# Half-width score products and an output one pair behind, in a gated linear attention with a squared-ReLU feed-forward

## The chip, the cores and the metric

One core of one Trainium2 chip runs the whole program in one launch. The metric is the device time of that core in microseconds (us). Engine names are those of the profile: PE is TensorE (PEld its weight loads), DVE is VectorE, ACT is ScalarE, POOL is GpSimd, SP issues the DMAs.

## The reference

```python
# q, k, v, alpha: (4 batches, 8 heads, 768 steps, 48), fp32; alpha in 0.8..1
for t in range(768):
    state = alpha[:, :, t, :, None] * state + einsum('bhd,bhe->bhde', k[:, :, t], v[:, :, t])
    y[:, :, t] = einsum('bhd,bhde->bhe', q[:, :, t], state)
x = y.transpose(0, 2, 1, 3).reshape(3072, 384)
h = maximum(x @ w_in, 0)          # w_in 384 x 2048, given in 64-bit floats
out = h * h @ w_out               # w_out 2048 x 384
```

The recurrence is computed by blocks of 128 steps of one batch (24 blocks: block n is batch n % 4, chunk n // 4). With b the running product of alpha in the block, q is multiplied by b and k by 1/b; then y = q·S + (masked scores)·v, where S is the state before the block, the scores are k against q, and the mask keeps a step's own and earlier steps. The new state is (S + sum of k·v) times the last b.

## The kernel before

Blocks go in six groups of four; a group's x is then 384 x 512 and goes through both layers of the feed-forward. Group 0 is computed in an opening, written out step by step. The attention of group g+1 is woven between the matmuls of group g's second layer (for group 1: between both layers of group 0). `weave` runs the list of feed-forward units in order and puts an attention step in front of the first unit whose time (a sum of unit costs) has reached the step's. In the groups from 1 on, the second layer has 28 units of four products each.

A head has 48 columns, two heads fill 128 rows as two halves of 64 (`e` = 0, 1), four such pairs `p`. From block 4 on, the scores of a block leave out one square of 64 x 64 (later keys against earlier queries): the first 64 keys meet all 128 queries, the last 64 keys only the last 64. The products use quarters of the PE array (64 rows x 64 columns). So that all four quarters work, the halves of some heads are swapped in place, and v is also loaded with its halves exchanged (`w`, 40 small DMAs). In the listing `chunks` and `halves_of_s` place the pieces; `sc` are the scores, `am` the masked copy to SBUF, `y` the output with the state sums `kv`, `st` the state, and `ev` copies y to x.

```python
    def bank(n, name, shape=(NP, C)):
        if n < GB and name in ("sc", "y"):
            return ps_ffn.tile([128, *shape], FP32, tag="f", name=name)
        return ps_att.tile([128, *shape], FP32, tag="att", name=name)
# ...
    def sc(n):
        ps = blk[n]["sc"] = [bank(n, "sc") for _ in range(2)]
        ks, qs = blk[n]["ks"], blk[n]["qs"]
# ...
        for x in range(2):
            for i in range(2):
                for p in (x, NP // 2 + x):
                    for e in range(2):
                        half = halves_of_s(p, i)
                        rows = slice(64 * e, 64 * e + D)
                        t = slice(64 * i, C)
                        nc.tensor.matmul(
                            out=chunks(ps[e].rearrange("a p t -> a (p t)"), half, p, i),
                            lhsT=ks[rows, p, 64 * i : 64 * (i + 1)], rhs=qs[rows, p, t],
                            start=True, stop=True, skip_group_check=True,
                        )
# ...
    def am(n):
        ps = blk[n].pop("sc")
# ...
        for e in range(2):
            o, data = (
                x.rearrange("a p t -> a (p t)")[:, 0 : 3 * C].rearrange("a (x k) -> a x k", x=2)
                for x in (am_t[n % NAM][:, e], ps[e])
            )
            mask = parts.rearrange("a k t -> a (k t)").bitcast(U32)
            nc.vector.copy_predicated(
                out=o, mask=mask.unsqueeze(1).to_broadcast(list(o.shape)), data=data
            )
# ...
    def y(n):
        ns, ys = [n, n + 1], [bank(n, "y", (2, NP // 2, C)) for _ in range(2)]
# ...
        heads = [(m, p, e) for m in ns for p in range(NP) for e in range(2)]
        for m in ns:
            blk[m]["y"] = ys
        for m, p, e in heads:
            if m // B:
                rows = slice(64 * e, 64 * e + D)
                product(m, p, e, s_t[m % B][rows, p, 0 : D + G * e], blk[m]["qs"][rows, p, :])
        if n < GB:
# ...
        for phase in range(2):
            for m in ns:
                for i in range(2):
                    for row in (1 - phase, phase) if (m, i) == (ns[0], 0) else (0, 1):
                        e = row ^ phase
                        for p in range(NP):
                            half = halves_of_s(p, i)
                            if half.start != 64 * row:
                                continue
                            x, h = "v", 2 * p + e
                            if p >= NP // 2:
                                x, h = "w", h - H // 2
                            cols = slice(h * D - G * e, (h + 1) * D)
                            ins = product(
                                m, p, e, tiles[x][m % len(tiles[x])][half, cols],
                                chunks(
                                    am_t[m % NAM][:, e].rearrange("a p t -> a (p t)"), half, p, i
                                ), slice(64 * i, C),
                            )
                            order("y", ins, phase)
            pass_on("y")
            for m in ns:
                if m // B == NCH - 1:
                    continue
                if phase == 0 and m == n:
                    kv = [bank(n, "kv", (2, NP // 2, 64)) for _ in range(2)]
                    begun = set()
                for p in range(NP):
                    half = slice(64 * (p % 2 ^ phase), 64 * (p % 2 ^ phase) + 64)
                    for e in range(2):
                        first = (2 * p + e) * D - G * e
                        ins = nc.tensor.matmul(
                            out=kv[p % 2][64 * e : 64 * (e + 1), m % 2, p // 2, :],
                            lhsT=tiles["k"][m % 4][half, 2 * p + e, :],
                            rhs=tiles["v"][m % NV][half, first : first + 64],
                            start=(p % 2, e) not in begun, stop=True, skip_group_check=True,
                        )
                        begun.add((p % 2, e))
                        order("kv", ins, phase)
                blk[m]["kv"] = kv
# ...
        else:
            s = s_t[n % B]
            for x in range(2):
                o = s[:, x::2, :]
                nc.vector.tensor_tensor(out=o, in0=src[x][:, n % 2], in1=o, op=ALU.add)
            nc.vector.tensor_tensor(
                out=s, in0=s, in1=last_t[n % 4].unsqueeze(2).to_broadcast([128, NP, 64]),
                op=ALU.mult,
            )
```

Between the two phases of `y` the rows of the array change the PSUM bank that they write; the `passed` instruction, an empty one on POOL, makes the second phase wait for the first. `ps_att` has four PSUM banks for the attention, taken in turn: a step that asks for a bank waits until the step four banks before it has been read.

The schedule:

```python
    PLAN = (
        (0.0, "ln0 ln1"),
        (2.0, "cs0 eb0 ei0"),
        (3.5, "cs1 mk0 eb1 ei1"),
        (5.0, "mq0 mq1 mk1"),
        (6.0, "kT0 kc0 bl0 bl1"),
        (7.0, "qT0 qc0 qT1 qc1"),
        (8.0, "kT1 kc1 br0 br1"),
        (10.0, "sc0 sc1 am0"),
        (11.0, "am1"),
        (12.0, "y0 ev0 st0 st1"),
    )
# ...
    def attention(g, begin, scale):
        out = []
        for at, fs in PLAN:
            for f in fs.split():
                for t in begin:
                    n = GB * g + 2 * begin.index(t) + int(f[-1])
                    out.append((t + at * scale, steps[f[:-1]], (n,)))
                    if f[:-1] == "qT" and n + 2 < NBLK:
                        out.append((t + at * scale, load, (n + 2, "aq")))
# ...
    def weave(units, events):
        at = 0
        for cost, f, args in units:
            while events and events[0][0] <= at:
                _, e, given = events.pop(0)
                e(*given)
            f(*args)
            at += cost
        for _, e, given in events:
            e(*given)
# ...
    units += [(1, ffn_out, (0, t, i)) for i in range(NW) for t in range(GB)]
    events = [(4.0 * i, next_weights, ()) for i in range(2 * NW)] + [(0, load, (GB + 1,))]
    events += [(47 + 2 * r, sum_w_in, (r,)) for r in range(NR2 - 1)]
    events += attention(1, (2.0, 27.0), 2.1)
    events += [(53, sum_x, (1,)), (54, sum_w_in, (NR2 - 1,))]
    weave(units, sorted(events, key=lambda x: x[0]))
    for g in range(1, NG):
        for j in range(NJ // 2 + 1):
            for i, step in enumerate("ABacCDd"):
                if j - step.islower() in range(NJ // 2):
                    ffn_in_pair(g, j - step.islower(), step)
# ...
        if g + 1 < NG:
            events = attention(g + 1, (0, 12.0), 1) + [(NU - 3, sum_x, (g + 1,))]
        weave([(1, ffn_product, (g, *divmod(u, NR2))) for u in range(NU)], events)
```

## Time and profile before

| | |
|---|---|
| time, median of 3 runs | 575.7 us (575.4 to 576.33) |
| span of the profiled execution | 573.2 us |
| PE, DVE, ACT busy | 560.3, 327.6, 222.8 us |
| opening (group 0's attention), to about 38 us | PE busy 29.9 of 38 |
| both layers of group 0 with group 1's attention | 38.2 to 132.3 us |
| first layer of each later group | 38.0 us each |
| second layer with attention, groups 1, 2, 3, 4 | 52.9, 52.9, 52.9, 51.7 us |
| second layer of group 5, no attention | 36.4 us |
| DMA | 38.94 MB, of it 1.9 MB the exchanged v |

The stretches are read off the chain of work that ended last, in order of time: its pieces are start, length, engine, tile, line and the number of instructions. In this trace one product in fp32 is two instructions, so "o x16" are eight products. A group of instructions by shape gives the busy time and the mean of one; because products in different quarters overlap, a mean is a latency there, and the pace has to be taken from the length of a piece divided by its instructions.

### The profile page before, as it was taken

To read this page: it belongs to the slowest core of one execution; us is meant where nothing else is said; L and a number is where in the kernel's file an instruction comes from. 1 tells how busy PE (TensorE), PEld (TensorE's weight loads), DVE (VectorE), ACT (ScalarE), POOL (GpSimd) and SP (SyncE) were. 2 spreads that over 40 slices of the span, in tenths; PEclk is the share of its full clock that TensorE was granted. 3 is DMA by queue.
4 is the path that set the end of the run, shared out by engine and by line. 5 is a ranking of instruction groups with operands and counts; after the bars stand their busy time and mean duration, and the time that the engine had idled before them with its cause. 6 is when DMAs were issued, how large, how long until landed. Compare 5 with 4: busy or idle time off the path is not lost.

```text
span 573.2 us, 11429 instructions
## 1 busy us (share of the span) xinstructions
PE 560.3 (98%) x4756; PEld 481.0 (84%) x4756; DVE 327.6 (57%) x653; ACT 222.8 (39%) x493; POOL 4.5 (1%) x29
## 2 busy tenths in 40 slices
PE   8789999999999999999999999999999999999996
PEld 6654565668889999889999888999988999988996
DVE  4988669875874534664534565652566443366430
ACT  4459865432344323334343234242333432333100
POOL 3000000000000000000000000000000000000000
PEclk9999999999999999999999999999999999999999
DMA  9986557621003335000454000435200340100001
GB/s 166 251 187 188 147 126 248 125 42 56 1 1 56 72 56 125 1 0 16 79 91 98 29 0 2 84 57 102 67 1 1 61 65 1 56 1 1 1 1 55
DMA packets 127963, 38.94 MB, mean 68 GB/s; under 512 B 119700, under 2 KB 122792, under 8 KB 127912
## 3 DMA queue, kind: packets, MB, share of 16 engines
q1 hardware_dynamic: 127912, 38.22, 30.5%
q8 instruction: 37, 0.61, 0.5%
q14 instruction: 14, 0.11, 0.1%
HBM read 33.45 MB, written 4.75 MB: 67 GB/s over the span
## 4 chain that ended last, share of the span: by engine, by line
PE 96%; DVE 2%; DMA 1%; issue 0%; ACT 0%; SPq 0%; POOL 0%; POOLq 0%
PE h L649 33%; PE o L720 32%; PE o L686 7%; PE h L611 7%; PE y L416 5%; PE cs L260 3%; PE sc L349 3%; PE qT L303 2%; PE kT L303 2%; PE kv L490 1%; DMA raw<-in_moe_w_in_dram 1%; PE warm L232 1%; PE sc L335 0%; DVE xT L514 0%; PE kv L393 0%
## 5 line engine op out<-in xcount | busy, mean ns | idle before, releaser
L649 PE MATMUL h<-xT,w_in 128*128 128x256 f32 x480 | 124.0, 379 | 0.0
L649 PEld LDWEIGHTS h<-xT,w_in 128*128 128x128 f32 x480 | 91.1, 190 | 12.3
L720 PE MATMUL o<-w_out,hid 128*128 128x192 f32 x480 | 83.3, 327 | 0.0
L720 PEld LDWEIGHTS o<-w_out,hid 128*128 128x128 f32 x480 | 78.7, 190 | 3.7
L514 ACT COPY xT<-y 32x256 f32<-32x256 f32 (+2 forms) x132 | 46.2, 364 | 77.1 <-PE y L416 73.5
L662 DVE TENSOR_TENSOR hid<-h,u 128x256 f32<-128x256 f32 x120 | 50.8, 424 | 28.9 <-PE h L649 25.0
L667 ACT ACTIVATE hid<-hid 128x256 f32<-128x256 f32 x40 | 16.7, 417 | 114.6 <-DVE hid L662 114.6
L662 DVE TENSOR_TENSOR u<-h,u 128x256 f32<-128x256 f32 x80 | 33.8, 423 | 35.3 <-PE h L649 22.9
L649 PE MATMUL h<-s3x,ws 128*128 128x256 f32 x160 | 47.6, 379 | 0.0
L611 PE MATMUL h<-xT,w_in 128*128 128x512 f32 (+1 forms) x108 | 43.6, 550 | 3.3 <-ACT xT L514 1.8
L384 DVE COPY_PREDICATED am<-parts,sc 128x384 f32<-128x384 uint32 x40 | 20.6, 577 | 45.7 <-PE sc L349 45.6
L686 PE MATMUL o<-w_out,hid 128*128 128x384 f32 x128 | 42.9, 489 | 0.0
L720 PE MATMUL o<-t,s 128*128 128x192 f32 x240 | 42.4, 328 | 0.0
L649 PE MATMUL h<-s3x,w_in 128*128 128x256 f32 x160 | 41.1, 379 | 0.0
L720 PEld LDWEIGHTS o<-t,s 128*128 128x128 f32 x240 | 39.0, 190 | 1.3
L611 PEld LDWEIGHTS h<-xT,w_in 128*128 128x128 f32 x108 | 19.8, 190 | 22.4 <-issue 16.3
L686 PEld LDWEIGHTS o<-w_out,hid 128*128 128x128 f32 x128 | 23.9, 190 | 15.6
L649 PEld LDWEIGHTS h<-s3x,ws 128*128 128x128 f32 x160 | 30.4, 190 | 4.1
L649 PEld LDWEIGHTS h<-s3x,w_in 128*128 128x128 f32 x160 | 30.4, 190 | 4.1
L720 PE MATMUL o<-t,hid 128*128 128x192 f32 x160 | 27.9, 329 | 0.0
L669 DVE SCALAR_TENSOR_TENSOR hid<-hid 128x512 f32<-128x512 f32 x40 | 27.2, 681 | 0.0
L720 PEld LDWEIGHTS o<-t,hid 128*128 128x128 f32 x160 | 25.8, 190 | 0.3
(109 smaller groups left out, 759.2 us busy)
## 6 DMA issues: line engine op xcount, KB each, us to landing
raw<-in_moe_w_in_dram SPq DMA_DIRECT2D x8, 768.0 KB, 5.5
raw<-in_moe_w_out_dram SPq DMA_DIRECT2D x8, 768.0 KB, 4.6
k_in<-in_k_dram SPq DMA_DIRECT2D x24, 192.0 KB, 5.0
out_dram<-osb SPq DMA_DIRECT2D x24, 192.0 KB, 2.1
v_in<-in_v_dram SPq DMA_DIRECT2D x23, 192.0 KB, 5.0
a_in<-in_alpha_dram SPq DMA_DIRECT2D x22, 192.0 KB, 3.6
q_in<-in_q_dram SPq DMA_DIRECT2D x22, 192.0 KB, 3.9
vx_in<-in_v_dram SPq DMA_DIRECT2D x40, 48.0 KB, 2.5
```

What stands on the lines that cost most here:

```text
L260: nc.tensor.matmul(out=ps.rearrange("a p t -> a (p t)")[:, 0 : H * D], lhsT=causal, rhs=blk[n].pop("la"), start=True, stop=True,)
L303: nc.tensor.transpose(out=ps[:, p, :], in_=rows[:, 128 * p : 128 * (p + 1)], identity=ident)
L349: nc.tensor.matmul(out=chunks(ps[e].rearrange("a p t -> a (p t)"), half, p, i), lhsT=ks[rows, p, 64 * i : 64 * (i + 1)], rhs=qs[rows, p, t ...
L384: nc.vector.copy_predicated(out=o, mask=mask.unsqueeze(1).to_broadcast(list(o.shape)), data=data)
L416: ins = nc.tensor.matmul(out=slot(ps)[64 * half : 64 * half + D + G * e, t], lhsT=lhsT, rhs=rhs, start=key not in seen, stop=True, skip_gr ...
L514: copy(out=x[to : to + m, kk, t : t + 2], in_=blk[n]["y"][e][r : r + m, :, p // 2],)
L611: nc.tensor.matmul(out=ps, lhsT=w[:, kk, c0 : c0 + 128], rhs=xT[g][:, kk, cols], start=(kk == 0), stop=(kk == KM - 1),)
L649: nc.tensor.matmul(out=ps, lhsT=a, rhs=b, start=(step.isupper() and i == 0), stop=(i == len(pairs) - 1), skip_group_check=True,)
L662: nc.vector.tensor_tensor(out=o, in0=ps, in1=z, op=ALU.add)
L669: nc.vector.scalar_tensor_tensor(out=h2, in0=h2, scalar=0.0, in1=h2, op0=ALU.max, op1=ALU.mult)
L686: nc.tensor.matmul(out=acc[t][:, 0:DM], lhsT=hid[i][:, j, t * C : (t + 1) * C], rhs=w_out[i][:, j, :], start=(i == 0 and j == 0), stop=(i ...
L720: nc.tensor.matmul(out=acc[k][:, t, :], lhsT=lhs[:, j, t * C : (t + 1) * C], rhs=rhs[:, j, :], start=(first and r + j + t == 0), stop=(r = ...
```

## The change

From block 4 on:

- The scores are computed as two squares on the diagonal only (16 products of 64 columns a block, where there were 8 of 64 and 8 of 128; the square of later keys against earlier queries was left out already). What the first 64 steps give to the last 64 now goes through the state: `u` = S + the sum of k·v over the first half, and the last 64 queries are multiplied with `u`, the first 64 with S. So q·S is split into two products of 64 columns, and the sums of k·v are kept apart by halves, in the last blocks too, where only the first half is needed.
- The output of a pair of blocks is computed one step behind: `ga(a, n)` does scores, sums, mask and state of block n and then the first part of the output of the pair a = n-2; one unit later `gb` does the rest of a's output, then the same for block n+1, then `ev`. The state is no longer updated in place but in tiles that rotate. Where there is no pair behind (after group 0's end), only the first part runs; a "last" slot does only the output.
- The pairs are spread differently: three slots beside group 0's layers (the third with output only), three pairs beside group 1's second layer, and two slots beside each of the next three, the last of which has output only. The scores of blocks 12 and 13, for instance, move from beside group 2 to beside group 1.
- v's exchanged copy and its DMAs go; v gets a fourth buffer, k has three, the logarithm is taken in place.
- In the opening, three products of a zero tile (128 x 256 each, into a bank that the scores of block 2 then overwrite) are put in front of `kv1`, for which PE waits.

The purpose is less PE work for the same output, with the output's inputs ready a whole slot early. The core of the diff, with cuts:

```diff
-    s_t = kept("s", B, [128, NP, 64])
+    s_t = [p2.tile([128, NP, 64], FP32, tag="s", name="s", bufs=B + 2) for _ in range(B)]
...
+    NV = 4
     tiles = {
...
+        "k": kept("k_in", 3, [128, H, 64]), "v": kept("v_in", NV, [128, H * D]),
     }
...
-    lent = {("a", 2): flat(tsum[0][0]), ("a", 3): flat(tsum[0][1]), ("v", 3): flat(tsum[0][2])}
-    for n in (2, 3):
-        t = lent["q", n] = flat(w_out[4 + n])[:, 0 : 64 * H].rearrange("a (h d) -> a h d", h=H)
+    lent = {("a", 2): flat(tsum[0][0]), ("a", 3): flat(tsum[0][1])}
...
-            if x == "v" and n >= GB:
-                t = tiles["w"][n % 2].rearrange("a (h d) -> a h d", d=D)
-                for i in range(2):
-                    s0 = c * C + (1 - i) * C // 2
-                    nc.sync.dma_start(
-                        out=t[64 * i : 64 * (i + 1)],
-                        in_=v[b, H // 2 :, s0 : s0 + C // 2, :].rearrange("h s d -> s h d"),
-                    )
     raws = {}
...
+    def zeros(n):
+        blk[n]["sc"] = [bank(n, "sc") for _ in range(2)]
+        for _ in range(3):
+            nc.tensor.matmul(
+                out=blk[n]["sc"][0][:, 0:2, :], lhsT=s_t[3].rearrange("a p d -> a (p d)")[:, 0:128],
+                rhs=s_t[3].rearrange("a p d -> a (p d)"), start=True, stop=True,
+            )
     def sc(n):
-        ps = blk[n]["sc"] = [bank(n, "sc") for _ in range(2)]
...
+        blk[n]["y"] = ys
+        def product(m, p, e, lhsT, rhs, t=slice(0, C)):
+            half = e ^ p % 2
+            ins = nc.tensor.matmul(
+                out=ys[e][64 * half : 64 * half + D + G * e, m % 2, p // 2, t], lhsT=lhsT, rhs=rhs,
+                start=(half, e) not in seen, stop=True, skip_group_check=True,
+            )
+            seen.add((half, e))
+            return ins
+        return product
...
+    def scores(n):
+        ps = two[n] = [bank(n, "sckv", (2, NP, 64)) for _ in range(2)]
+        ks, qs = blk[n]["ks"], blk[n]["qs"]
+        for p in range(NP):
+            for h in range(2):
+                for e in range(2):
+                    rows = slice(64 * e, 64 * e + D)
+                    nc.tensor.matmul(
+                        out=ps[e][HALF[h], 0, p, :], lhsT=ks[rows, p, HALF[h]],
+                        rhs=qs[rows, p, HALF[h]], start=True, stop=True, skip_group_check=True,
+                    )
+    def masked(n):
+        ps = two[n]
+        if n // 2 < GB // 2 + NAM and n % 2 == 0:
+            nc.gpsimd.memset(am_t[n // 2 % NAM], 0.0)
+        for e in range(2):
+            nc.vector.copy_predicated(
+                out=am_h(n)[:, e, n % 2], data=ps[e][:, 0],
+                mask=halves_mask.bitcast(U32).unsqueeze(1).to_broadcast([128, NP, 64]),
+            )
+    def am_h(n):
+        t = am_t[n // 2 % NAM].rearrange("a e p t -> a (e p t)")
+        return t.rearrange("a (e m p t) -> a e m p t", e=2, m=2, p=NP)
+    def state_sums(n):
+        ps = two[n]
+        for p in range(NP):
+            for e in range(2):
+                first = (2 * p + e) * D - G * e
+                for h in range(1 if n // B == NCH - 1 else 2):
+                    nc.tensor.matmul(
+                        out=ps[h][64 * e : 64 * (e + 1), 1, p, :],
+                        lhsT=tile_of("k", n)[HALF[h], 2 * p + e, :],
+                        rhs=tiles["v"][n % NV][HALF[h], first : first + 64],
+                        start=True, stop=True, skip_group_check=True,
+                    )
+    def sums_copied(n):
+        ps = two.pop(n)
+        u = blk[n]["u"] = p2.tile([128, NP, 64], FP32, tag="us", name="us", bufs=3)
+        nc.vector.tensor_tensor(out=u, in0=ps[0][:, 1], in1=s_t[n % B], op=ALU.add)
+        blk[n]["kv1"] = ps[1][:, 1]
+    def next_state(n):
+        blk[n]["s"] = s_t[n % B]
+        if n // B < NCH - 1:
+            s = s_t[n % B] = p2.tile([128, NP, 64], FP32, tag="s", name="s", bufs=B + 2)
+            last = last_t[n % 4].unsqueeze(2).to_broadcast([128, NP, 64])
+            nc.vector.tensor_tensor(out=s, in0=blk[n].pop("kv1"), in1=blk[n]["u"], op=ALU.add)
+            nc.vector.tensor_tensor(out=s, in0=s, in1=last, op=ALU.mult)
...
+    def inner(product, m, p, e, h):
+        head = 2 * p + e
+        return product(
+            m, p, e, tiles["v"][m % NV][HALF[h], head * D - G * e : (head + 1) * D],
+            am_h(m)[HALF[h], e, m % 2, p, :], HALF[h],
+        )
...
+    def ga(a, n):
+        if n is not None:
+            for f in (scores, state_sums, masked, sums_copied):
+                f(n)
+        if a is not None:
+            product = y_begin(a)
+            for h in range(2):
+                for m, p, e in heads(a):
+                    rows = slice(64 * e, 64 * e + D)
+                    s = blk[m]["u" if h else "s"]
+                    product(m, p, e, s[rows, p, 0 : D + G * e], blk[m]["qs"][rows, p, HALF[h]], HALF[h])
+            for m, p, e in heads(a):
+                end = inner(product, m, p, e, e)
+            passed = nc.gpsimd.nop(nofuse=True)
+            dep(passed, end)
+            two["y"] = product, passed
+        if n is not None:
+            next_state(n)
+    def gb(a, n):
+        if a is not None:
+            product, passed = two.pop("y")
+            for i, (m, p, e) in enumerate(heads(a)):
+                begin = inner(product, m, p, e, 1 - e)
+                if i == 0:
+                    dep(begin, passed)
+        if n is not None:
+            for f in (scores, state_sums, masked, sums_copied, next_state):
+                f(n + 1)
+        if a is not None:
+            ev(a)
+            for m in (a, a + 1):
+                blk[m].clear()
     def ev(n):
...
+        weights1 y0 cs3 ev0 br1 kT2 qT2 zeros2 ei3 kc2 qc2 kv1 eb3 mk3 load4v kT3 first0
         st0 mq3 weights2 load4q load4k middle0 sc2 kc3 qT3 second0 qc3 bl3 am2 br3 st1 br2
         kv2 sc3 am3 ha0 first1 ha1 middle1 y2 ev2 load4a hb0 first2 hb1 second1 st2 kv3
...
-        (0.0, "ln0 ln1"),
+        (0, "ln0"),
+        (0.5, "ln1"),
         (2.0, "cs0 eb0 ei0"),
-        (3.5, "cs1 mk0 eb1 ei1"),
-        (5.0, "mq0 mq1 mk1"),
-        (6.0, "kT0 kc0 bl0 bl1"),
-        (7.0, "qT0 qc0 qT1 qc1"),
-        (8.0, "kT1 kc1 br0 br1"),
-        (10.0, "sc0 sc1 am0"),
-        (11.0, "am1"),
-        (12.0, "y0 ev0 st0 st1"),
+        (3.0, "cs1 eb1 ei1"),
+        (3.5, "mk0"),
+        (4.0, "bl0"),
+        (4.5, "mq0 mk1 bl1"),
+        (5.0, "mq1"),
+        (6.5, "qT0 qc0 qT1 qc1 kT1 br1"),
+        (7.5, "kc1"),
+        (8.0, "kT0 kc0 br0"),
+        (9.5, "ga"),
+        (10.5, "gb"),
     )
...
     units += [(1, ffn_out, (0, t, i)) for i in range(NW) for t in range(GB)]
-    events = [(4.0 * i, next_weights, ()) for i in range(2 * NW)] + [(0, load, (GB + 1,))]
+    events = [(4.0 * i, next_weights, ()) for i in range(2 * NW)]
+    events += [(0, load, (GB + 1,)), (1.0, load, (GB + 2, "k"))]
     events += [(47 + 2 * r, sum_w_in, (r,)) for r in range(NR2 - 1)]
-    events += attention(1, (2.0, 27.0), 2.1)
+    events += attention([(0, GB, False), (18.0, GB + 2, True), (27.5, GB + 4, True, True)], 2.35)
     events += [(53, sum_x, (1,)), (54, sum_w_in, (NR2 - 1,))]
     weave(units, sorted(events, key=lambda x: x[0]))
     for g in range(1, NG):
...
         if g + 1 < NG:
-            events = attention(g + 1, (0, 12.0), 1) + [(NU - 3, sum_x, (g + 1,))]
+            n = GB * (g + 1) + 2
+            pairs = [(0, n, True), (13.5, n + 2, True)]
+            if g == 1:
+                pairs = [(0, n - 2, False), (7.0, n, True), (14.0, n + 2, True)]
+            events = attention(pairs, 1) + [(NU - 3, sum_x, (g + 1,))]
         weave([(1, ffn_product, (g, *divmod(u, NR2))) for u in range(NU)], events)
```

## The prediction

> **What bounds the kernel now.** I read the page first: how busy is each engine?
>
> ```profile
> PE 560.3 (98%) x4756; PEld 481.0 (84%) x4756; DVE 327.6 (57%) x653; ACT 222.8 (39%) x493; POOL 4.5 (1%) x29
> ```
>
> PE is busy in 98% of the span. Then the waits of PE alone: if it nearly never waits, only less PE work can shorten the program.
>
> ```profile
> PE h L611 <- ACT xT L514: 1.8, 3, 1.3
> PE kv L393 <- DVE ks L319: 1.8, 1, 1.8
> PE kT L303 <- DVE k_in L278: 1.3, 1, 1.3
> PE warm L232 <- POOL s L79: 1.1, 1, 1.1
> PE h L611 <- DVE am L371: 0.9, 1, 0.9
> PE qT L303 <- DVE w_out L278: 0.7, 1, 0.7
> PE h L611 <- DVE w_in L188: 0.6, 1, 0.6
> PE y L416 <- DVE am L371: 0.2, 1, 0.2
> ```
>
> All of these lie before 38.3 us (the list for the window from 38 us on has only the 0.6). From then to the last output PE stands in a queue of its own work. So the change is priced in PE time, piece by piece. The pieces are in the chain in order of time (start, length, engine, tile, instructions); one pair beside group 1's second layer:
>
> ```profile
> 183.69 2.60 PE o L720 x16
> 186.30 1.50 PE sc L349 x64
> 187.79 2.80 PE o L720 x16
> 190.59 1.70 PE y L416 x63
> 192.29 0.47 PE kv L490 x32
> 192.76 0.66 PE y L416 x32
> 193.42 0.47 PE kv L490 x32
> 193.89 2.80 PE o L720 x16
> 196.69 0.65 PE cs L260 x2
> ```
>
> The reader is to see three things. First, sixteen feed-forward instructions take 2.60 us, but 2.80 after a stretch of quarter-array products: coming back costs **0.20 us**. Second, the quarter products of 64 columns run at 0.47/32 = **14.7 ns an instruction** (`kv`). Third, those of 128 columns cost twice as much: `y` has 95 instructions listed (one record is missing), 64 of 128 columns and 32 of 64, so 64 x 29.4 + 32 x 14.7 = 2.35 us, against 1.70 + 0.66 = 2.36 measured. `sc` has 32 of each: 1.41 us, against 1.50 measured; I call the 0.09 left the price of going in.
>
> The means by shape must not be taken for the pace:
>
> ```profile
> L490 PE MATMUL kv<-v_in,k_in 64*64 64x64 f32 x512 | 10.6, 218 | 0.0
> L349 PE MATMUL sc<-qs,ks 48*64 48x128 f32 x320 | 14.5, 277 | 0.0
> ```
>
> 218 ns is the latency of one of many that overlap; the pace is 14.7.
>
> **What the Trainium skill says.** "TensorEngine Tiling (Array Packing)", Key Properties: changing the tiling mode drains the engine. The trace agrees in that 2.60 becomes 2.80. The same page, Gotcha 1: different row tiles cannot access one PSUM bank at the same time. That is why both kernels put a `passed` between the two parts of y; no run here shows what happens without it. "TensorE: Matmul & The Clock Gate", Part 1: after an idle window of about 3.4 us PE falls to half its clock. This is what the zero products guard against. The trace shows half pace only at the start (the warm-up products of 256 columns, 654 ns on average, against 379 for such products later). The hole of 1.8 us does not cost it: `kv` of block 0 and block 2 take 1.03 us for 8, `kv1` right after the hole 1.13, `sc` before and after 1.16 for 16. Nothing to win there.
>
> **The change part by part.** A pair is two blocks.
>
> 1. A pair before: `sc` 1.50, return 0.20, y and kv 1.70 + 0.47 + 0.66 + 0.47 = 3.30, return 0.20. Sum **5.20 us**.
> 2. A pair after, every product with 64 columns and two instructions: scores 2 blocks x 16 products x 2 = 64 instructions; sums 64; state products 16 heads x 2 halves x 2 = 64; inner products 64. Together 256 x 14.7 ns = 3.76 us. There are again two stretches (`ga`, `gb`), so 2 x 0.20 and once 0.09: **4.25 us**. The gain is in two terms: scores 1.41 to 0.94 and inner products 1.41 to 0.94. State products (0.94) and sums (0.94) stay. Ordinary pair: 0.95 us less. Eight such pairs (blocks 4 to 19): -7.6 us.
> 3. The last two pairs (blocks 20 to 23) had no sums before. The chain shows y there at 463.16 us as 1.73 and at 464.98 as 0.89, so 2.71 with the gap; 1.50 + 0.20 + 2.71 + 0.20 = 4.61 us. The change adds sums for the first half: 32 instructions a pair, but on one half of the rows, so two quarters of four, twice the price, and 0.94 us again. After: 4.25. Gain 0.36 x 2 = -0.7 us.
> 4. Extra stretches. Before, five groups x 4 = 20. After, three slots beside group 0, three beside group 1, two beside each of three more: 12 slots x 2 = 24. Four more at 0.20 + 0.09: +1.2 us.
> 5. The rest (transposes, cumulative sums, feed-forward) is the same number of instructions, only moved. The zero products: 6 instructions of 256 columns, at 2.60/16 = 162 ns per 192 columns about 217 each, 1.3 us in a hole that ends 1.8 us after the last qT: fits, 0.
> 6. DVE per block, before: two masked copies of 384 elements at 577 ns, two adds at 283, one product at 425: 2.15 us. After: two masked copies of 256, three tensor operations of 256 at 425. The masked copy is 577 ns at 384 elements and 722 at 512, so 432 at 256 (my estimate from those two). 0.86 + 1.28 = 2.14 us. DVE neither gains nor loses. ACT does the same work. 1.9 MB of small DMAs go, in a program that waits for no DMA after the opening.
>
> Sum: -7.6 - 0.7 + 1.2 = **-7.1 us**, which gives 568.6.
>
> By stretch: both layers of group 0 from 94.0 to about 92.7 us (two pairs less 1.9, two stretches more 0.6); group 1's second layer from 52.9 *up* to 56.5, as it takes a third pair's front (cs 1.3, transposes 1.75 and scores and sums of 1.88); groups 2 and 3 52.9 to 51.0; group 4 51.7 down to 46.1, with one pair's front gone. First layers stay 38.0, the tail 36.4.
>
> **The rivals.**
>
> *A new wait in the dense slots.* Beside group 1 the pairs begin 7 units apart and not 12. `gb` asks for the two banks of `ga`'s scores again, so PE waits unless DVE has masked, added and read the second bank. From the start of `ga`: scores and sums 0.94 us, DVE's four operations behind it end at about 2.4 to 2.9. PE meanwhile has sums, y (1.41) and one unit (2.60/2 + 0.20) and the inner part (0.47): it gets there at 4.3. Without y to do (first slot) it has cs (0.65) instead: at 3.1. Thin but enough. At the end of group 1, `gb` falls on unit 25 of 28: the copies of x take about 12 x 0.364 = 4.4 us, and PE has scores and sums 0.94, the return and three units 3.9, together 5.0, before the first layer needs x. Before, it was four units. Beside group 0 DVE is already busy 33 of 44 us with the weights, in order, so one late operation delays the weights. And k of a block is asked for in `ga`, two units before it is scaled, and lands 5 us later (median): DVE can stall on it. The trace speaks for slack (no PE wait at all after 38.3 us), the plan against it. Each such miss is 0.5 to 2 us; if all came true, the time would be 573 to 575.
>
> *The pace of 14.7 ns does not hold* where 160 instructions with a new weight load each follow one another, or where rows of 48 are used. In y before, 95 + 64 such instructions ran back to back at that pace, so I expect it to hold. If every one cost 17 ns, each pair would lose 0.6 us and the gain would be about 1 us.
>
> *The returns are cheaper than I think.* If the four extra stretches cost nothing: 567.4.
>
> *A shorter opening*: with the exchanged v gone, SP issues the third weight tile 1.4 us earlier. But DVE works through the conversions without a break when PE waits for w_in at 38.2, so I give it nothing.
>
> **Range and chances.** I take 0.6 us of new waits, an estimate for one of the misses above: **569.2 us**. The range of 8 in 10 is 565.5 to 573.5: below, cheaper stretches and a shorter opening; above, several misses. Over 2% faster would be below 564.2, which needs two thirds more than the whole gain I can count: 0.05. Over 2% slower (above 587.2) needs a stall in every slot: 0.03. Within 2%: 0.92.
>
> **What will show it.** In the changed profile: scores, sums, state and inner products at 14.7 ns an instruction, a `ga` of about 2.35 us and a `gb` of about 1.4 with 0.2 behind each; second layers of 56.5, 51.0, 51.0, 46.1 us; PE without waits after 38.3 us; zero products ending before `kv1`'s input is there, and `kv1` where it was. I am wrong if PE waits for DVE or ACT at `sckv`, at `h` after group 1, or if the stretches are longer than their instructions say.

## The result, and the profile after

The changed kernel takes **572.75 us** (median of 3 runs, 572.41 to 572.76) against 575.7: ratio 0.9945, 95% interval 0.9922 to 0.9968. The span of the profiled execution goes from 573.2 to 570.8 us. It is faster by 2.4 to 3 us, less than half of the 6.5 forecast. So the sum of the prediction (-7.1 us in the span) missed by 4.7 us, and the task is to find these.

From the page of after, the line that answers to the one the prediction shows:

```profile
PE 558.5 (98%) x5146; PEld 477.1 (84%) x5146; DVE 326.9 (57%) x655; ACT 222.1 (39%) x493; POOL 5.8 (1%) x28
```

PE has 390 product instructions more (smaller ones; two make a product) and is busy 1.8 us less. DVE and ACT have not moved (327.6 and 222.8 before). So PE is still the bound, as forecast; but where the sum promised 7 us less PE work, there are two. The waits of PE in after from 38 us on (waited for: us in total, times, longest):

```profile
PE h L603 <- DVE w_in L178: 0.6, 1, 0.6
PE sckv L430 <- issue: 0.5, 1, 0.5
PE qT L291 <- DVE q_in L266: 0.3, 1, 0.3
```

The first was there before. The other two are new, and both are longer than this list says, as the chain will show.

The chain of after in order of time (start, length, engine, tile, instructions), one ordinary pair beside group 3's second layer:

```profile
372.40 0.62 PE sckv L404 x32
373.02 0.47 PE sckv L430 x32
373.49 1.40 PE y L380 x90
374.89 1.50 PE o L712 x8
376.39 0.62 PE y L380 x31
377.01 0.47 PE sckv L404 x32
377.48 0.47 PE sckv L430 x32
```

`ga` is 0.62 + 0.47 + 1.40 = **2.49 us** (forecast 2.35), `gb` 0.62 + 0.47 + 0.47 = **1.56** (forecast 1.4); the unit between them is 1.50, which is 1.30 and 0.20 for coming back. The first 32 instructions of each stretch take 0.62, all later ones 0.47: each stretch pays 0.15 us at its ends on top of the 0.20.

The same by stretch. The columns are the window, its length, then the busy time and count of PE, PEld, DVE, ACT and POOL, the granted clock, the DMA share and GB/s. The windows are the second layers of groups 1 to 4, from their first `o` to the first product of the next layer, in after:

```profile
169.66:227.94 58.28, 57.81 (x926) 53.75 (x925) 30.34 (x66) 24.66 (x58) 0.00 (x0) 1.00 0.47 90
265.92:318.21 52.29, 51.84 (x778) 49.38 (x776) 24.79 (x52) 19.88 (x48) 0.00 (x0) 1.00 0.37 70
356.19:407.60 51.41, 51.41 (x745) 49.09 (x744) 23.13 (x48) 19.88 (x48) 0.00 (x0) 1.00 0.34 67
445.59:492.07 46.48, 46.48 (x598) 44.73 (x597) 17.28 (x34) 15.10 (x38) 0.00 (x0) 1.00 0.03 10
```

Groups 2 and 3 have nearly the same work (group 3 has some sums less, worth 0.06 us), but group 2 takes 0.88 us more, and only part of that is idle PE. Forecast were 56.5, 51.0, 51.0 and 46.1. First layers stay at 37.99 and the products of the last layer at 36.41, as before.

Where group 2 loses it, in the chain of after:

```profile
286.74 0.47 PE sckv L404 x32
287.21 0.35 PE sckv L430 x21
287.56 0.45 issue
288.01 0.45 PE sckv L430 x11
```

A run of one kind of product, two thirds done, stops with nothing that it waits for in the profile ("issue"), and comes back slowly: 1.25 us for 32 sums that took 0.47 above.

And group 1, in the timeline of PE and of DVE (start, length, instruction, in brackets the idle time before it and its releaser; the first two lines are PE, the last two DVE):

```profile
195.04 0.63 PE L291 MATMUL qT<-ident,q_in 128*128 128x128 f32 x4
195.98 0.63 PE L291 MATMUL qT<-ident,q_in 128*128 128x128 f32 x4 [0.31 <-DVE q_in L266]
...
194.35 0.55 DVE L266 TENSOR_TENSOR q_in<-q_in,b 128x384 f32<-128x384 f32 x1
195.28 0.55 DVE L266 TENSOR_TENSOR q_in<-q_in,b 128x384 f32<-128x384 f32 x1
```

The scaling of q comes late because DVE is busy without a break from 190.9 us on: to 192.9 with the masks and states of `gb` of the pair in front, then with a scaling of k and two operations of the feed-forward. PE loses 0.50 us before the second transpose (0.94 from start to start, where 0.44 is usual) and, by the same reading, 0.27 before the first: 0.77 together.

### The profile page after: what moved, and what is told of

Same layout as the page of the kernel before. It is cut to its first block, busy times and chain, and to the rows that moved or that the text cites. A ratio compares the mean times of both kernels' runs of the same rounds, so it can differ in the third digit from the quotient of the medians.

```text
span 570.8 us, 12170 instructions
## 1 busy us (share of the span) xinstructions
PE 558.5 (98%) x5146; PEld 477.1 (84%) x5146; DVE 326.9 (57%) x655; ACT 222.1 (39%) x493; POOL 5.8 (1%) x28
## 4 chain that ended last, share of the span: by engine, by line
PE 95%; DVE 2%; DMA 1%; issue 1%; ACT 0%; SPq 0%; POOL 0%; DVEq 0%; POOLq 0%
PE h L641 33%; PE o L712 32%; PE o L678 7%; PE h L603 7%; PE y L380 4%; PE cs L248 3%; PE sckv L404 2%; PE kT L291 2%; PE sckv L430 2%; PE qT L291 2%; DMA raw<-in_moe_w_in_dram 1%; PE warm L220 1%; PE sc L333 0%; DVE xT L520 0%; PE kv L350 0%
## 5 line engine op out<-in xcount | busy, mean ns | idle before, releaser
L520 ACT COPY xT<-y 32x256 f32<-32x256 f32 (+2 forms) x132 | 46.1, 364 | 58.5 <-PE y L380 54.6
L414 DVE COPY_PREDICATED am<-halves_mask,sckv 128x256 f32<-128x256 uint32 x40 | 15.5, 441 | 55.8 <-PE sckv L430 55.8
L661 DVE SCALAR_TENSOR_TENSOR hid<-hid 128x512 f32<-128x512 f32 x40 | 27.3, 681 | 0.0
L746 DVE TENSOR_TENSOR osb<-o,us 128x384 f32<-128x384 f32 x10 | 5.6, 558 | 37.2 <-PE o L712 37.2
```

Of the source, the lines that this page charges most:

```text
L414: nc.vector.copy_predicated(out=am_h(n)[:, e, n % 2], data=ps[e][:, 0], mask=halves_mask.bitcast(U32).unsqueeze(1).to_broadcast([128, NP, ...
L520: copy(out=x[to : to + m, kk, t : t + 2], in_=blk[n]["y"][e][r : r + m, :, p // 2],)
L661: nc.vector.scalar_tensor_tensor(out=h2, in0=h2, scalar=0.0, in1=h2, op0=ALU.max, op1=ALU.mult)
```

## The experiments

The theory (A in the expectations) has three terms: each stretch of quarter products costs 0.35 us beyond its products; PE's instructions run out where very many come in a short time; in the dense slots of group 1 PE waits for DVE. Its rivals: the stops are the DMAs that `gb` starts, or an accident of one run; a stretch costs only the 0.20; or the gain is spent elsewhere (the zero products, the output behind the scores).

**1. The same kernel again.** No edit.

> The changed kernel once more, with more rounds, as the yardstick of the other runs. Both theories: 572.7 us, 0.9945 of the kernel before, with stops of PE in the middle of the quarter-array products of gb at the same places (0.27 us near 222.5 and 0.67 us near 288.0 of the span) if they belong to the program, at others if they are chance.

Measured: 572.07 us, ratio 0.9921 (0.9895 to 0.9947). The stops are at the same products again (at 222.0 us in y, at 286.9 in the sums), with other sizes (0.26 and about 0.08), and there is one of 0.37 at 311.8 that the first profile lacked. So they belong to the program; their size changes from run to run.

**2. `gb` two units after `ga`, beside the second layers.**

```diff
-                    w = t + at * scale
+                    w = t + (at + (f == "gb" and scale == 1)) * scale
...
-                pairs = [(0, n - 2, False), (7.0, n, True), (14.0, n + 2, True)]
+                pairs = [(0, n - 2, False), (7.0, n, True), (13.5, n + 2, True)]
```

> Two feed-forward units between ga and gb in place of one, beside the second layers. Theory A (PE runs out of instructions: they come in blocks of 256, and ga, one unit and gb are 528 instructions in 5.5 us): 256 instructions then take 1.3 us longer, no stop inside gb is left, and the 1.2 us of stops beside groups 1 and 2 go: about 571.5 us. Theory B (the stops come from something else, such as the loads of k and v issued at that place): the stops stay, 572.7.

Measured: 572.64 us, 0.9934 (0.9908 to 0.9960). An ordinary `ga` with y is 2.49 and `gb` 1.56, no stop anywhere: group 2 takes 51.37, group 3 51.31. The place beside group 2 where after stopped, in the chain of this run:

```profile
286.60 2.80 PE o L712 x16
289.40 0.62 PE y L380 x31
290.02 0.47 PE sckv L404 x32
290.49 0.47 PE sckv L430 x32
```

The same number of instructions, spread over one unit more, run without a stop. But group 1 takes 59.36, because the second pair now gives back its banks later. The waits of PE in this run:

```profile
PE qT L291 <- ACT xT L520: 1.2, 1, 1.2
```

The transposes of the third pair want a bank of y that ACT has not yet copied to x. The whole gain of 1.1 us in groups 2 to 4 was given back in group 1. The forecast of the time was missed for that reason.

**3. The transposes of q one unit later, beside group 1 only.**

```diff
-    def attention(pairs, scale):
+    def attention(pairs, scale, late=0):
...
             for at, fs in PLAN:
+                at += late if "qT0" in fs else 0
...
-            events = attention(pairs, 1) + [(NU - 3, sum_x, (g + 1,))]
+            events = attention(pairs, 1, g == 1) + [(NU - 3, sum_x, (g + 1,))]
```

> Only beside group 1, the transposes of q and of one k are done one unit later. Theory A (in the dense slots DVE, which has the masks and states of one pair to do, is late with the scaled q of the next, and PE stands for 0.8 us before two transposes at 195 and 196 us): the waits go, 572.0 us. Theory B (DVE stays that late whatever the place, because it is busy until then): the wait moves to the next product, 572.7.

Measured: 572.18 us, 0.9918 (0.9892 to 0.9944). The wait for `q_in` is gone from the list of waits, and group 1 takes 57.94 instead of 58.28, less of a gain than the 0.77 removed, because the stops were larger in this profile (0.57 at 222.7, 0.17 at 207.8). Another part was lost before 40 us; it comes up at the end.

**4. y in a stretch of its own.** As in 2, and the first part of y is moved one unit behind the scores and sums of `ga`, so seven slots have three stretches and not two.

```diff
+            for f in (scores, state_sums, masked, sums_copied, next_state):
                 f(n)
+    def gy(a, n):
         if a is not None:
             product = y_begin(a)
...
+                        if f == "ga":
+                            out.append((w + (scale == 1), gy, given))
```

> As gb_later, and the output part of ga is put one unit after its scores, so that seven slots have three stretches of quarter-array products and not two. Theory A (each stretch costs 0.35 us beyond its products: 0.2 at the two changes and 0.15 inside at its ends): 7 x 0.35 = 2.45 us more than gb_later. Theory B (my prediction's 0.20, and 0.09 more at times): 1.4 to 2.0 us more.

Measured: 575.31 us, 0.9976 (0.9963 to 0.9990): 2.67 us more than run 2 for seven stretches with no product added, 0.38 each. A's 0.35 gives 2.45; one stop of about 0.3 in this profile (at 290.8, in the sums of `gb`) may fill the gap. The chain of this run:

```profile
284.41 0.47 PE sckv L430 x32
284.88 1.50 PE o L712 x8
286.37 1.56 PE y L380 x92
```

y by itself is 1.56, and 1.40 where it follows other quarter products: the 0.15 at the ends is real, and comes with every stretch.

**5. The instruction count shifted.** The six instructions of the zero products are replaced by 80 small ones in the same hole, so all later PE instructions stand 148 further on (each of the 80 and of the 6 comes with a weight load of its own).

```diff
-        for _ in range(3):
-            nc.tensor.matmul(
-                out=blk[n]["sc"][0][:, 0:2, :], lhsT=s_t[3].rearrange("a p d -> a (p d)")[:, 0:128],
-                rhs=s_t[3].rearrange("a p d -> a (p d)"), start=True, stop=True,
-            )
+        for i in range(40):
+            e, c = i % 2, i // 2 % 2
+            rows = slice(64 * e, 64 * e + 64)
+            nc.tensor.matmul(
+                out=blk[n]["sc"][e][64 * c : 64 * c + 64, 0, 0:64], lhsT=s_t[3][rows, 0, :],
+                rhs=s_t[3][rows, 1, :], start=True, stop=True, skip_group_check=True,
+            )
```

> The three zero products of the opening are replaced by 40 zero products of 64 columns on quarters of the array, which take about as long (80 x 14.6 ns = 1.2 us) but are 160 instructions and not 12. All later PE instructions so move by 148 against the blocks of 256. Theory A (stops come where PE enters a block of instructions that has not arrived): the stops of 0.67 us and 0.37 us inside gb beside group 2 and the slow ends of gb beside group 1 are no longer at the same products (state sums of gb); where two blocks are crossed in 3.2 to 3.4 us after a longer pause I expect none or under 0.3 us, in all about 1 us less than the changed kernel: 571.5. Theory B (a wait for data or for the loads issued there): same products, same stops, 572.5.

Measured: 572.32 us, 0.9926 (0.9900 to 0.9952). The stops moved to other products: the one near 222 us from y to the sums (0.49 at 224.3), the one near 287 from the sums to y (0.12), and there is one in group 3, where there was none before (0.14). Counted from the records (each product instruction with its weight load, and PE's own semaphore instructions), every stop of this run and of all others lies at 192 to 198 of a count modulo 256. So place right; but I had expected the stops to shrink more, and about 0.75 us of them was left.

**6 and 7. The output not behind.** Half scores and state products as in the change, but the pair's two score steps in one stretch and its own output 2.5 units later, in the slots that the kernel before had. In the first of the two runs the schedule also put ACT's logarithm for the next pair behind its copies of x; the second run only moves the second slot of each group by a thousandth of a unit, which turns that order round.

```diff
+    def two_scores(n):
+        for m in (n, n + 1):
+            for f in (scores, state_sums, masked, sums_copied, next_state):
+                f(m)
+    def two_outputs(n):
+        ga(n, None)
+        gb(n, None)
...
-        (10.5, "gb"),
+        (12.0, "gb"),
...
-                        out.append((w, {"ga": ga, "gb": gb}[f], given))
+                        out.append((w, {"ga": two_scores, "gb": two_outputs}[f], (n0,)))
...
-    events += attention([(0, GB, False), (18.0, GB + 2, True), (27.5, GB + 4, True, True)], 2.35)
+    events += attention([(2.0, GB, False), (27.0, GB + 2, False)], 2.1)
...
-            pairs = [(0, n, True), (13.5, n + 2, True)]
+            pairs = [(0, n, False), (12.0, n + 2, False)]
```

(In the second of them 12.0 is 11.999 in the last line.)

> Half scores and split state as in the change, but the output in the same slot as its scores, in the slots of the kernel before: scores and sums of both blocks in one stretch, the whole output in another, two to three units later. Theory A (the lag is there because u and the masked scores must have come from DVE, 4.3 us of work for a pair): PE waits for DVE before each output, and for POOL between the parts of the output, some 0.3 to 1 us a pair; four stretches less save 1.4 us; beside group 1 the DVE wait of 0.8 us goes, as the pairs are 12 units apart: 572 to 578 us, with waits of y for DVE in the list. Theory B (the lag is not needed, two units cover DVE): 571 us, no waits.

Measured: 585.32 us, 1.0152 (1.0123 to 1.0180): a miss. 8.6 us are PE waiting at the cumulative sums for ACT's logarithm (`cs` for `a_in`), my order, not the idea.

> As not_behind, with one step moved: the logarithms of the second pair are put ahead of the copies of x of the first on ACT, where the run before had them behind and PE stood 8.6 us for them. Theory A (what is then left against the changed kernel is 0.33 us for each passing between the two parts of the output, ten times, less four stretches of 0.35 us and less the stops and the DVE wait): about 574 us. Theory B (DVE is not ready with u and the masks two units after the scores): waits of PE y for DVE, 576 or more.

Measured: 575.61 us, 1.0000 (0.9988 to 1.0012). That wait is down to 1.1, no stops, no wait of y for DVE. What is left in the chain of this run, between the two parts of y:

```profile
307.32 1.59 PE y L380 x91
308.92 0.02 issue
308.94 0.03 POOLq L485
308.97 0.04 issue
309.01 0.69 PE y L380 x31
309.70 5.40 PE o L721 x32
```

The passing instruction on POOL is now uncovered: from the first part to the second it is 1.69, then 0.69 to the return, where `ga` and `gb` bury it under a unit. By starts of products I read 0.33 us a pair. A pair takes 2.02 + 2.38 + 2 x 0.20 = 4.80 against 4.45 behind and 5.20 before. So without the output one step behind, **0.35 of the 0.75 us** that an ordinary pair gains in the change would be lost again: it is not the readiness of y's inputs (nothing waited for them here), it is the hidden passing. That is no gain over the kernel before, which hid the passing too, under the 0.47 us of `kv` between the two parts of y; with those sums moved to the scores, something else has to cover it. Half scores alone, in the old slots, were worth nothing measurable: eight ordinary pairs gain 3.2 us, the last two lose 0.4, and the waits for `a_in` (1.1) and `w_out` (0.7), with slower cumulative sums behind the first (0.91 for two, 0.65 elsewhere), take the rest.

**8. The loads of `gb` two units later.**

```diff
-                                out.append((w, load, (m, x)))
+                                out.append((w + 2 * scale, load, (m, x)))
```

> The loads of v, and of one k, that were asked for in gb are asked for two units later (in group 0's part scaled likewise). Theory A (the stops are a matter of how long PE takes for 256 instructions; a fetch shares the DMA engines with these loads, but its own time is 0.9 to 1.5 us with or without them): stops at the same places, 572.5. Theory B (the loads hold up the fetch): the stops shrink to nothing, 571.3.

Measured: 572.0 us, 0.9931 (0.9905 to 0.9958). Stops at the same places of the count (0.18 at 286.6, 0.40 at 311.5), none near 222. The loads are not what stops PE; whether they lengthen a stop is open, as the sizes vary by as much between two runs of one kernel.

**9. Without the zero products.** `zeros2` is dropped from the opening.

> The changed kernel without the three zero products of the opening; nothing else. Theory A (the hole they fill ends when DVE has copied k, 0.5 us after them, and a hole of 1.8 us does not slow PE): the same time, 572.1 to 572.7, and the opening's products as fast as with them. Theory B (they keep PE from falling to half its pace in some executions): now and then up to 1.3 us more, with products of 256 columns at 430 ns an instruction between 27 and 39 us of the span.

Measured: 572.36 us, 0.9940 (0.9921 to 0.9959), a median among those of the runs with them. `kv1` starts at 20.17 us, in after at 20.16. So at the median they cost nothing and bring nothing. But one of the 11 executions took 575.54 us, with a granted clock (the share of its full clock that PE was granted, on average) of 0.988. Of the 62 executions of the kernel before in these rounds 15 show such a clock (0.988 to 0.990) and take 578.3 to 579.2 us, about 3 us over the others; of the 79 executions with filler products in that place (run 5's among them) none lies under 0.994. This speaks for Theory B, with 3 us and not 1.3; one execution in 11 doesn't settle it, and no profile was taken of such an execution. The medians of before that the ratios here are taken against hold these executions too.

**10. The best of these.** Transposes of q one unit later for group 1's second pair only, and `gb` two units after `ga` only from group 1's third pair on.

```diff
+            second = scale == 1 and n0 == 2 * GB + 2
+            later = scale == 1 and n0 > 2 * GB + 2
             for at, fs in PLAN:
+                at += "qT0" in fs and second
...
+                at += fs == "gb" and later
...
-                pairs = [(0, n - 2, False), (7.0, n, True), (14.0, n + 2, True)]
+                pairs = [(0, n - 2, False), (7.0, n, True), (13.5, n + 2, True)]
```

> Both mendings where they fit: the transposes one unit later for the second pair beside group 1 only; gb two units after ga in the slots from that group's third pair on. Theory A: of the changed kernel's losses the DVE wait of 0.8 us and stops of about 1 us go, and the wait of 1.2 us for x's copies that gb_later had does not come, as that pair's gb is left in place: 570.6 us. Theory B (each mending is paid back elsewhere, as in the two runs before): 572.

Measured: **571.07 us** (570.58 to 571.76), 0.9904 (0.9883 to 0.9925), the fastest of all; span 568.9. The second layers of groups 1 to 3 of this run, columns as above:

```profile
169.62:227.19 57.57, 57.35 (x925) 53.45 (x924) 30.36 (x66) 24.48 (x58) 0.00 (x0) 1.00 0.48 91
265.18:316.55 51.37, 51.37 (x777) 49.05 (x776) 24.87 (x52) 19.89 (x48) 0.00 (x0) 1.00 0.37 71
354.54:405.85 51.31, 51.31 (x746) 48.98 (x744) 23.19 (x48) 19.89 (x48) 0.00 (x0) 1.00 0.34 67
```

Group 2 is 0.92 us shorter than in after and PE is busy throughout it. A wait for `q_in` remains in group 1, now before the third pair (0.2 in the list, 0.55 by the starts of the products). 57.57 is 0.71 less than after.

**11. Two stretches joined.** Run 10, with both score steps of group 1's first pair in one stretch and the last output in one go.

```diff
+                if scale == 1 and not after:
+                    at = 10.5 if fs == "ga" else at
+                if scale == 1 and n0 >= NBLK:
+                    at = 9.5 if fs == "gb" else at
```

> As best, and two half-empty slots lose a stretch: beside group 1 the scores of the first pair's two blocks follow each other without a unit between, and beside group 4 the last output is done in one go. Theory A: each saves 0.35 us; the output in one go shows what passing from the first part to the second costs when nothing covers it (my guess 0.2 to 0.4 us): 570.2 us. Theory B: the joined scores wait for banks until ACT has read the sums of logs, up to 1 us: 571.

Measured: 571.18 us, 0.9905 (0.9882 to 0.9928): no gain over run 10. The last output in one stretch is 2.38 with 0.33 of passing uncovered, which is what the saved stretch was worth; in group 1 the joined scores give DVE a later start, and PE waits twice for `q_in` (0.5 in all), so group 1 takes 57.70.

## Why the prediction was wrong

**The bound: right.** PE is the bound before and after, DVE did not move (step 6: 2.14 us a block forecast, 2.15 measured, as before; the masked copies were 441 ns, not the 432 estimated), first layers and tail stayed, the zero products end 0.47 us before `kv1` (step 5), which starts at 20.16 us, at 20.17 without them (run 9) and at 19.95 in before:

```profile
18.23 1.46 PE L320 MATMUL sc<-s 128*128 128x256 f32 x6
20.16 1.13 PE L350 MATMUL kv<-v_in,k_in 128*128 128x96 f32 x8 [0.47 <-DVE ks L307]
```

(The timeline of PE in after.)

**Step 1: right.** 5.20 us for a pair before is measured, not assembled.

**Step 2: mis-sized, the largest part.** Forecast 4.25 for a pair, measured 4.45. The direction and the products were right; the price of going in was wrong. It was charged once a pair (0.09) and is paid in every stretch (0.15), twice a pair: the prediction's own sign of being wrong, stretches longer than their instructions say. The check that let it pass was y: 64 x 29.4 + 32 x 14.7 = 2.35 "against 2.36 measured". It held two errors that cancelled: a 128-column product is not twice a 64-column one. The old y's second part, in the midst of a stretch, ran 16 of each in 0.66 us, so (0.66 us - 16 x 14.7 ns)/16, about 27 ns (27.3 by the starts of the state products in before, four in 109 ns), and y is 64 x 27.3 + 32 x 14.7 = 2.22 with 0.15 for its ends. With 27.3, `sc` is 0.87 + 0.47 + 0.15 = 1.49 (1.50 measured). So the halving gains less, and the ends cost more. Eight pairs at -0.75 instead of -0.95: 1.6 us.

**Step 3: mis-sized for the same reason.** The last pairs are 2.43 + 1.64 + 0.40 = 4.47 and not 4.25, a gain of 0.14 each and not 0.36: 0.4 us. The argument on the half sums (half the instructions at twice the price) held.

**Step 4: right in kind, small in size.** Four stretches more, at 0.35 instead of 0.29: 0.2 us. Run 4 measured 0.38 with a stop in it. "The Trainium skill", page "TensorEngine Tiling (Array Packing)", Key Properties, says that a change of mode drains the engine; the 0.35 us a stretch agrees with that, and no run here parts the drain from the rest of it.

Steps 2 to 4 together: **2.2 us** of the 4.7.

**The rival "a new wait in the dense slots": partly true.** It named the right engine and the right group, and put the wait at the wrong place. The banks of `ga` were ready in time, as it worked out; `h` after group 1 did not wait. What waited was the transpose of q, since the scaling of q queues behind the four operations of `gb`: **0.77 us**. This is about the 0.6 us given for such a miss.

**The rival "the pace does not hold": true, but not in the form given.** The pace of 14.7 ns holds wherever nothing stops it (though the 95 + 64 instructions that the prediction took as its proof are not all at that pace: 64 of them have 128 columns). What was not named is that PE runs short of instructions. In after it costs **1.4 us** as read off the starts of products around the stops. The difference to run 10 gives 1.6: 0.9 in group 2, 0.5 in group 1 (less the waits for `q_in`, 0.77 and 0.55), 0.1 each in groups 3 and 4. What speaks for it: the page lists a queue for instructions, here in after, in before and in run 5, which has 148 instructions more than after:

```profile
q8 instruction: 40, 0.66, 0.5%
q8 instruction: 37, 0.61, 0.5%
q8 instruction: 41, 0.67, 0.5%
```

These are packets of 16 KB. At 256 instructions each, the 40 and 37 hold 10,240 and 9,472, nearly PE's own count (a product instruction and a weight load for each of the 5146 and 4756). All stops lie at one place of a count modulo 256; 148 more instructions ahead of them moved them to other products at that same place (run 5), and with 12 fewer they lie there too (run 9: 0.27 at 287.3, 0.28 at 312.1); moving the loads did not move them (run 8); the same instructions spread over one unit more have none (runs 2 and 10). `ga`, a unit and `gb` are 2 x (160 + 8 + 96) = 528 instructions in 5.5 us.

The records of these packets tell more. Paired in order with the blocks of 256, over all profiles, PE passes from one block to the next inside quarter products 225 times, and never sooner than 1.23 us after the packet of the new block has landed. Each of the 13 stops of over 0.1 us ends 1.27 to 1.54 us after its packet; where PE comes to that place more than 1.5 us after the packet, nothing over 0.06 us is left of a stop. So, as far as these records go, a stop is as long as its packet is late: in after the packet landed at 286.60 and PE, there at 287.34, went on at 288.01. Most stops follow 256 instructions gone through in some 3.4 us (one of 0.17 us follows 4.0); at 4.7 and more there was none. But it isn't the pace alone: blocks gone through in 1.9 to 2.7 us, behind one of 10 us or more, have no stop, since their packets had been fetched earlier. "The Trainium skill", page "Runtime: NRT & Kernel Launch", section Instruction fetch mechanics, says that instructions come in blocks of 16 KiB, 256 each, and that crossing costs little, "mostly hidden". The first half agrees with the runs. The second holds for most of this program, and not for `ga` and `gb` one unit apart, where a crossing cost up to 0.8 us. What fills the 1.3 us between the landing and the next instruction, and why a packet is asked for sooner in one run than in another, stays open.

**The opening: 0.35 us.** The first layer's later start (38.58 against 38.23) is no effect of the change: in the eleven further profiles it lies between 38.1 and 39.7, also where the opening's code is the same.

The sum: -7.1 + 2.2 + 1.4 + 0.77 + 0.35 = -2.4 us, the difference between the spans of the two profiled executions; 0.2 of it may belong to the sizes or to the stops. The medians differ by 2.95; both lie within the interval of the ratio.

## What to carry to other kernels

When a count of equal pieces is checked against one measured length, check it against two of different make-up: a pace that is too high and a fixed cost that is left out hide each other in a single sum. Price small quarter-array products by stretch as well as by instruction, here 0.35 us a stretch, and cover the passing between two row halves with other work: bare, it cost 0.33 us a pair here, nearly half of what the narrower products gain. And where products become smaller and more, ask how fast the instructions can arrive: spreading two dense stretches over one unit more removed stops that no engine's work and no load of data explained.

## What was not expected of the hardware

- **Instruction supply.** Stops on PE of up to 0.8 us with the slow return, always at 192 to 198 of a count of its instructions modulo 256, and ending some 1.3 to 1.5 us after a packet of instructions has landed.
- **Half the columns is not half the time.** Quarter products of 64 columns start every 14.7 ns, those of 128 every 27.3.
- **The first layer at half pace.** In three of eleven further profiles (runs 3, 7 and 11), eight products of 256 columns near 35 us took as long as in the first line (run 3); the second is run 10, as elsewhere (the timeline of PE); the third has the stretch of half clock in run 3 (columns as in the tables of windows, the granted clock third from the end):

```profile
34.79 3.33 PE L603 MATMUL h<-xT,w_in 128*128 128x256 f32 x8 [0.19 <-ACT xT L520]
35.05 1.99 PE L603 MATMUL h<-xT,w_in 128*128 128x256 f32 x8 [0.19 <-ACT xT L520]
35.28:38.69 3.41, 3.41 (x11) 2.79 (x11) 3.35 (x6) 1.30 (x4) 0.00 (x0) 0.50 1.00 344
```

  "TensorE: Matmul & The Clock Gate", Part 1 of the Trainium skill, ties half a clock to an idle window of about 3.4 us. Here the holes ahead of it are 1.3 us and less, one after another, and PE is busy for 1.89 of the 3.41 us just before the half clock in run 3, so the runs don't match the page's condition. All three have the zero products in the opening: these do not prevent this one.
